# Decay rows laid out chunk by chunk, and another order of the opening, of the loads and of two blocks

## The chip, the cores and the metric

The kernel runs on one core of a Trainium2 chip. The metric is device time in microseconds (us) of one execution; lower is better. A core has five engines with queues of their own: TensorE (PE; its weight loads are shown apart as PEld), VectorE (DVE), ScalarE (ACT), GpSimd (POOL) and SyncE (SP), which here only issues DMAs. Line numbers are those of the kernel before.

## The reference

A Mamba-2 scan over 32 pairs of batch and head (4 batches, 8 heads, 768 tokens, 32 channels, 16 states), followed by a feed-forward layer with a maximum over three products. The scan is written with chunks; what one chunk computes, with `cum` the running sum of the logarithms of `a`:

```python
L = np.exp(cum[:, :, :, None] - cum[:, :, None, :]) * causal
M = np.einsum('bhin,bhjn->bhij', Cc, Bc) * L
y = np.einsum('bhij,bhjd->bhid', M, xc) \
  + np.einsum('bhin,bhnd->bhid', Cc, state) * np.exp(cum)[:, :, :, None]
state = decay_full * state + np.sum(Bx, axis=2)
...
x = y.transpose(0, 2, 1, 3).reshape(3072, 256)
h = np.maximum(np.maximum(x @ w1, x @ w2), x @ w3)      # 3072 x 768
out = h @ w_out                                         # 3072 x 256
```

## The kernel before

**Tiling.** The kernel cuts the 768 tokens into 6 chunks of 128 tokens. One chunk of all four batches is 512 columns of the feed-forward part. Chunk c's scan gives `y`, 256 channels by 512 tokens, which is the feed-forward input of chunk c. The scan of chunk c+1 is put between the feed-forward matmuls of chunk c. All matmuls of one engine run in the order in which the program writes them; that order is written out by hand as strings of one-letter words.

**The opening** (the string before line 997) does chunk 0's scan. `C0`, `B0`, `C1`, `B1` transpose halves of C and B (two batches each), `c` and `b` copy them, `i`, `j`, `v` and `u` build the exponent of the decay on TensorE, GpSimd and VectorE, `e` takes its exponential on ScalarE, `s` makes scores, `x` and `z` multiply them with the decay on VectorE, `y` does so for two heads groups through a ScalarE copy and GpSimd (`aside_product`, L894 and L896), `o0` and `o2` make the two halves of y (`first_own`, L631), `A` and `S` the state. `P` is a dummy matmul that keeps TensorE busy. `k`, `l` and `r` clip, take logarithms and sum `a` for all chunks, and `r` ends with `store_sums`, which writes the running sums to the DRAM tensor `cums`. `W` fetches the next of 12 weight pieces of 512 KB, `X0` and `X1` ask for B and C of chunk 1, `L` for its decay rows, `E` for its end-of-chunk rows. `G` and `H` are the two halves (L679) of the first two feed-forward groups.

**The first feed-forward part** (loop `for n in range(NF * 3)`, strings FIRST) has 18 groups in plain float32, two per weight piece; groups 0 and 1 are the halves of the opening, groups 2 to 17 are two matmuls each (L687). A group's result is copied (L1170) or goes into a maximum (L1174). Each weight piece is first decoded (`d`: two ScalarE steps L220 and L229, two VectorE steps L221 and L224, one GpSimd addition L230; `g`: the sign, VectorE L233). Behind group n the words of FIRST[n] are issued: `b` and `t` transpose B and C of the next chunk (TensorE, L511), `C` and `c` make C's copies (L530) and its product with the exponential `E` (L541, after ScalarE's L534), `s0` and `s2` make scores, `p0` takes four pieces of the decay's exponential (ScalarE, L485), `x` multiplies scores with decay (VectorE, L596), `m` masks the decay rows on GpSimd (L478), `w` splits a weight piece for the later, three-term products (L267, L269, L273 or L277, L262), and `M` issues a load: `M10` and `M11` the two decay loads of chunk 1, `M6`, `M7`, `M8` its B, C and x, `M9` its E; `M0`, `M1`, `M2` B, C and x of chunk 2, `M3` its E, `M4` and `M5` its decay loads. `scan_tc` has 32 dummy matmuls (L520) ahead of chunk 1's transposes of C.

**The seam** (SEAM, PRELUDE) makes y of chunk 1 (`scan_own`: 32 matmuls with the state, L611, then 64 with the decayed scores, L620) and splits it into three terms (L647, L650, L661).

**Blocks one to five** have 18 units each (`unit`): two opening matmuls (L728), a scaling of the bank by ScalarE (L714), four main matmuls (L750), then a copy (`COPIES` says which on ScalarE, the others on VectorE, L762) or a maximum (L764). `unit_open` opens units ahead; the units in `LATE` open the next one after their main matmuls, the others before. Block one (SECOND) also has chunk 0's down projections (`D`, L787) and the scan of chunk 2; blocks two to four (STEADY) have down projections L792; block five (LAST) has no scan left.

**Loads.** All loads but three small ones of `a` go through SP's queue, in program order. The program gives DMAs eight semaphores in turn, and each DMA waits for the one eight places ahead of it. C has one buffer, B and x two each, the decay tiles L two; weight pieces and the split weights share twelve. A decay load copies rows of two batches to all 128 partitions; E is loaded by eight DMAs, one per head:

```python
cums = dram.tile([BH, NC, P], FP32, name="cums")
...
nc.sync.dma_start(
    out=L[:, b:b + 2].rearrange("j b h i -> j (b h) i"),
    in_=cums[b * NH:(b + 2) * NH, c, :].partition_broadcast(P))
```

Of the kernel before, what the change touches and what calls it, by code (L numbers as in the profile page):

```python
# [9 lines left out]
FP32 = mybir.dt.float32  # L10
# [10 lines left out]
def kernel(  # L21
# [55 lines left out]
    COPIES = {c: (1, 6, 7,) if c == 1 else (1, 13,) for c in range(1, NC)}  # L77
    LATE = {c: (2, 3, 5, 8, 10, 14, 16, 17,) if c == 1 else (1, 3, 4, 6, 7, 9, 11, 14, 16, 17,) for c in range(1, NC)}
    WEIGHTS_DVE = ((0, 1), (1, 2), (2, 1), (3, 1), (4, 1), (5, 2), (6, 1), (7, 1), (8, 1), (10, 2), (11, 1), (11, 2),)
# [223 lines left out]
    for word in "W B0 C0 B1 C1 W W x0 x1".split():  # L303
        if word == "W":
            fetch()
        else:
            load_half(word[0], int(word[1]))
# [153 lines left out]
    cums = dram.tile([BH, NC, P], FP32, name="cums")  # L461

    def decay_load(c, pairs=(0, 2)):
        L = decays(c) if 0 in pairs else Ls[c]
        for b in pairs:
            nc.sync.dma_start(
                out=L[:, b:b + 2].rearrange("j b h i -> j (b h) i"),
                in_=cums[b * NH:(b + 2) * NH, c, :].partition_broadcast(P))

    def last_load(c):  # L470
        E = blocks[c]["E"] = raw.tile([HN, NB, P], FP32, tag="E", bufs=2, name="E")
        rows = cums[:, c].rearrange("(b h) s -> h b s", h=NH)
# [42 lines left out]
    def scan_tc(c, kind):  # L515
        st = blocks[c]
        st["trC"] = tr = kind([HN, NB, P], "trC")
        if c == 1:
            for _ in range(32):
                nc.tensor.matmul(  # L520
                    out=tr[:, 0, :64], lhsT=ident16[:, :HN], rhs=mask[:, :64], start=True, stop=True)
# [376 lines left out]
    def store_sums():  # L898
        nc.sync.dma_start(
            out=cums.rearrange("k c s -> (k c) s").rearrange("(w r) s -> r w s", w=2), in_=a_sb)  # L900
# [93 lines left out]
    for word in ("v3 q v2 d i0 j P P P P C0 k e01 e00 c0 J e11 i2 u2 B0 P P B1 b0 e10 P s0 g e20 l "  # L994
            "x0 P P C1 b1 i3 c1 x3 r u3 x2 e30 e31 x1 W P P P s2 s3 e21 D P P A X0 z0 y2 y3 "
            "o0 z1 n d o2 W W N G0 E W H0 G1 H1 S W").split():
        begin(word)
# [71 lines left out]
    def plan(words, c, n):  # L1069
# [9 lines left out]
        "g d",  # L1079
        "W g M10 M7 d",  # L1080
        "",
        "d g d W W",
        "W f",
        "M11 g w0,0 F M3 d M8 g w1,0 m0,0",
        "b",
        "",
        "M0 g",
        "d p0 d M1 t d C g",
        "p0",
        "m0,2 s0 E d",  # L1090
        "p0",
        "w1,1 g w0,1 M2 c M4 x M5",
        "x",
        "p0 x p0 p0 B x",
        "s2 p0 g d g x",
        "p0 w2,0 x x w0,2 x w3,0 g w2,1 w1,2 w2,2",
    ]
    SEAM = "y a z A a D z w3,1 x"
    PRELUDE = "b B w3,2"
    SECOND = [  # L1100
        "t w4,0 E w5,0 c w6,0 w4,1 L m0,0",
        "",
        "p0",
# [118 lines left out]
```

## Time and profile before

| What | us |
|---|---|
| median of 3 runs (lowest, highest) | 275.91 (275.49, 277.44) |
| the profiled execution | 275.21 |
| its span, first to last instruction | 273.5 |

By stage, in one answer of windows (busy us of each engine, granted TensorE clock as a share of full speed, mean busy share of the DMA engines):

| Stage | us from the start | PE | DVE | ACT | POOL | clock | DMA |
|---|---|---|---|---|---|---|---|
| opening | 0 to 21.4 | 18.8 | 10.6 | 12.3 | 8.9 | 1.00 | 0.87 |
| first feed-forward part and seam | 21.4 to 63.7 | 40.0 | 35.7 | 31.5 | 24.1 | 1.00 | 0.96 |
| block one | 63.7 to 102.3 | 38.4 | 26.1 | 33.4 | 26.0 | 1.00 | 0.75 |
| block two | 102.3 to 143.2 | 40.4 | 28.0 | 28.7 | 6.7 | 1.00 | 0.57 |
| blocks three and four | 143.2 to 223.7 | 80.5 | 53.2 | 55.1 | 7.5 | 1.00 | 0.26 |
| block five and the end | 223.7 to 273.5 | 46.6 | 28.8 | 20.6 | 0.0 | 1.00 | 0.07 |

Busy time of TensorE counts the overlapping ends of matmuls as busy, so a stage in which it is busy throughout has no idle time, but not every busy stage is at the peak. A chain of waits follows the end of the program back through what released each step. Idle time of an engine off that chain costs nothing.

### The profile page before, as it was taken

What the parts mean: (1) busy time and instruction counts of PE and PEld (TensorE: products, weight loads), DVE (VectorE), ACT (ScalarE), POOL (GpSimd) and SP (SyncE); (2) the same over time, 40 slices, a digit from 0 to 9 for tenths busy, and PEclk for the clock granted to TensorE, in tenths of its full rate; (3) what the DMA queues carried; (4) which work ended last, traced back from release to release, by engine and by line L of the source; (5) the groups of instructions that cost most, each with busy time, mean ns of one, the idle gap of its engine ahead of it and who ended that gap; (6) DMA issues with size and microseconds to landing.
All of it is one profiled execution on the core that took longest, in us unless ns stands there. A gap on an engine that the chain in (4) does not pass through costs nothing.

```text
span 273.5 us, 5483 instructions
## 1 busy us (share of the span) xinstructions
PE 264.7 (97%) x2100; PEld 206.7 (76%) x2100; DVE 182.4 (67%) x297; ACT 181.6 (66%) x413; POOL 73.0 (27%) x72
## 2 busy tenths in 40 slices
PE   6999999989999999999999999999999999999995
PEld 4566444448877788679888889788789788899894
DVE  2574979798556689862588861688761787732882
ACT  3768759963998998936689845699754564534711
POOL 4433566574949270133001133001000000000000
PEclk9999999999999999999999999999999999999999
DMA  5999799599993175994304794200000100002002
GB/s 123 176 193 224 245 240 312 117 110 213 288 250 57 50 94 75 153 250 41 99 19 40 141 230 53 79 2 0 0 4 29 49 2 2 0 0 79 0 0 77
DMA packets 105097, 28.13 MB, mean 103 GB/s; under 512 B 75376, under 2 KB 102000, under 8 KB 105072
## 3 DMA queue, kind: packets, MB, share of 16 engines
q1 hardware_dynamic: 104768, 27.66, 48.9%
q8 instruction: 16, 0.26, 0.4%
q10 hardware_dynamic: 304, 0.13, 0.2%
q14 instruction: 9, 0.07, 0.1%
HBM read 24.54 MB, written 3.24 MB: 102 GB/s over the span
## 4 chain that ended last, share of the span: by engine, by line
PE 81%; DVE 7%; ACT 5%; DMA 4%; issue 2%; POOL 1%; ACTq 0%; DVEq 0%; POOLq 0%
PE up L750 26%; PE up L728 13%; PE o L792 13%; PE up L687 6%; DMA raw_C<-in_C_dram 4%; PE s L588 4%; PE o L787 4%; PE y L620 3%; PE o L819 2%; PE spread L414 2%; ACT L L485 2%; PE y L611 2%; PE up L679 1%; PE up L914 1%; DVE L L596 1%
## 5 line engine op out<-in xcount | busy, mean ns | idle before, releaser
L750 PE MATMUL up<-six,wp 128*128 128x512 f32 x360 | 96.5, 396 | 0.5 <-ACT up L714 0.5
L750 PEld LDWEIGHTS up<-six,wp 128*128 128x128 f32 x360 | 66.0, 188 | 16.0 <-ACT up L714 1.4
L764 DVE TENSOR_TENSOR m<-m,up 128x512 f32<-128x512 f32 x60 | 40.4, 683 | 48.2 <-PE up L750 47.9
L714 ACT ACTIVATE up<-up 128x512 f32<-128x512 f32 x90 | 50.7, 581 | 26.7 <-PE up L728 25.5
L485 ACT ACTIVATE L<-L,ncums 128x128 f32<-128x128 f32 x160 | 50.3, 393 | 2.4 <-POOL L L478 2.3
L728 PE MATMUL up<-six,wd 128*128 128x512 f32 x180 | 51.7, 394 | 0.0
L728 PEld LDWEIGHTS up<-six,wd 128*128 128x128 f32 x180 | 33.1, 188 | 8.5 <-DVE m L764 1.0
L596 DVE TENSOR_TENSOR L<-s,L 128x512 f32<-128x512 f32 x46 | 30.3, 682 | 2.4 <-PE s L588 1.6
L478 POOL TENSOR_SCALAR_AFFINE_SELECT L<-L 128x1024 f32<-128x1024 f32 x20 | 22.7, 1161 | 26.8 <-DMA L<-cums 26.8
L687 PE MATMUL up<-six,w 128*128 128x512 f32 x64 | 28.7, 596 | 0.0
L792 PE MATMUL o<-wp,h 128*128 128x256 f32 x192 | 23.7, 283 | 0.0
L792 PEld LDWEIGHTS o<-wp,h 128*128 128x128 f32 x192 | 23.4, 192 | 0.1
L661 DVE SCALAR_TENSOR_TENSOR h<-h,h 128x512 fp32r<-128x512 f32 x30 | 21.5, 718 | 1.0
L687 PEld LDWEIGHTS up<-six,w 128*128 128x128 f32 x64 | 11.8, 190 | 13.1 <-issue 11.6
L667 ACT ACTIVATE h<-m 128x512 fp32r<-128x512 f32 x30 | 18.4, 628 | 3.6 <-DVE m L764 3.6
L670 DVE TENSOR_TENSOR h<-m,h 128x512 fp32r<-128x512 f32 x30 | 20.5, 683 | 0.1
L230 POOL TENSOR_TENSOR h<-h,h 128x512 uint32<-128x512 uint32 x12 | 16.7, 1392 | 13.9 <-DVE h L224 9.6
L762 DVE COPY m<-up 128x512 f32<-128x512 f32 x19 | 13.1, 688 | 9.8 <-PE up L750 9.6
L805 ACT ACTIVATE ob<-o 128x512 f32<-128x512 f32 x10 | 6.0, 598 | 19.9 <-PE o L792 16.2
L588 PE MATMUL s<-six,six 32*128 32x256 f32 x192 | 15.4, 401 | 0.0
L575 POOL TENSOR_TENSOR S<-S,old 128x256 f32<-128x256 f32 x4 | 2.9, 736 | 44.7 <-DVE S L567 44.7
L588 PEld LDWEIGHTS s<-six,six 32*128 32x128 f32 x192 | 9.7, 184 | 5.9 <-issue 3.1
(111 smaller groups left out, 324.2 us busy)
## 6 DMA issues: line engine op xcount, KB each, us to landing
L<-cums SPq DMA_DIRECT2D x10, 1024.0 KB, 10.0
rb<-in_moe_w_dram SPq DMA_DIRECT2D x9, 512.0 KB, 5.1
raw_x<-in_x_dram SPq DMA_DIRECT2D x5, 512.0 KB, 10.3
out_dram<-ob SPq DMA_DIRECT2D x10, 256.0 KB, 2.1
rb<-in_moe_w_out_dram SPq DMA_DIRECT2D x3, 512.0 KB, 7.1
raw_B<-in_B_dram SPq DMA_DIRECT2D x5, 256.0 KB, 5.7
E<-cums SPq DMA_DIRECT2D x40, 32.0 KB, 2.2
raw_C<-in_C_dram SPq DMA_DIRECT2D x5, 256.0 KB, 6.5
```

Of the source, the lines that this page charges most:

```text
L478: nc.gpsimd.affine_select(out=Ls[c][:, b], in_=Ls[c][:, b], pattern=[[0, NH], [1, P]], compare_op=ALU.is_ge, fill=MASKED, base=0, channel_ ...
L485: nc.scalar.activation(L[:, b, h], L[:, b, h], AF.Exp, bias=ncum[c][:, b * NH + h:b * NH + h + 1], scale=1.0)
L588: nc.tensor.matmul(out=s[:, i].rearrange("j g i -> j (g i)"), lhsT=st["BT"][rows, b], rhs=st["CT"][rows, :, b], start=(i == 0), stop=True, ...
L596: nc.vector.tensor_tensor(out=M, in0=s, in1=M, op=ALU.mult)
L661: nc.vector.scalar_tensor_tensor(out=out, in0=lo.bitcast(FP32), scalar=-1.0 / TAU, in1=hi.bitcast(FP32), op0=ALU.mult, op1=ALU.add)
L670: nc.vector.tensor_tensor(out=lo, in0=src, in1=hi.bitcast(FP32), op=ALU.subtract)
L687: nc.tensor.matmul(out=bank, lhsT=whole[3 * (f // 2) + i][:, k, f % 2 * P:(f % 2 + 1) * P], rhs=yT[0][:, k], start=(k == 0), stop=(k == KD ...
L714: nc.scalar.activation(bank, bank, AF.Copy, scale=-KAPPA)
L728: nc.tensor.matmul(out=o, lhsT=weight_part(k, 2, kk, cols), rhs=yT[c][2][:, kk], start=(kk == 0), stop=(kk == KD - 1), skip_group_check=True)
L750: nc.tensor.matmul(out=o, lhsT=weight_part(k, j, kk, cols), rhs=yT[c][j][:, kk], start=False, stop=(kk == KD - 1 and j == 1), skip_group_c ...
L764: nc.vector.tensor_tensor(out=m[g], in0=m[g], in1=o, op=ALU.max)
L792: nc.tensor.matmul(out=o[:, b % 2], lhsT=hs[f][p][:, tokens(b)], rhs=weight_part(NW + f // 2, p, f % 2, slice(0, DM)), start=(first and p ...
```

## The change

`cums` is laid out chunk by chunk, so that what one decay load reads is one run of 8 KB instead of 16 rows of 512 bytes; it is stored by two DMAs instead of one. The order of the first loads changes (C ahead of B, x ahead of two of the first four weights). The opening, FIRST, the seam and SECOND get other orders: C of chunk 1 is asked for in the opening, right after B and one weight; its two decay loads follow four weights later, E of chunk 1 comes behind eleven weights and both decay loads, and then one decay load, the last weight, x of chunk 1, B, C, x and the second decay load of chunk 2, and its E. The transposes of chunk 1's B go ahead of group 2, those of C behind group 4. The 32 dummy matmuls of `scan_tc` are gone; the opening has 13 dummies (`P`) instead of 14. Which units open late, which copies go to ScalarE and which weight splits to VectorE changes too; STEADY and LAST keep their words.

```diff
-    COPIES = {c: (1, 6, 7,) if c == 1 else (1, 13,) for c in range(1, NC)}
-    LATE = {c: (2, 3, 5, 8, 10, 14, 16, 17,) if c == 1 else (1, 3, 4, 6, 7, 9, 11, 14, 16, 17,) for c in range(1, NC)}
-    WEIGHTS_DVE = ((0, 1), (1, 2), (2, 1), (3, 1), (4, 1), (5, 2), (6, 1), (7, 1), (8, 1), (10, 2), (11, 1), (11, 2),)
+    COPIES = {c: (7, 12,) if c == 1 else (1, 12, 13,) for c in range(1, NC)}
+    LATE = {c: (3, 5, 9, 10, 11, 13, 15, 16,) if c == 1 else (1, 3, 4, 6, 7, 8, 10, 12, 13, 14, 16, 17,) for c in range(1, NC)}
+    WEIGHTS_DVE = ((0, 1), (1, 1), (2, 1), (3, 1), (4, 1), (6, 1), (6, 2), (7, 1), (8, 2), (9, 1), (10, 1), (10, 2),)
...
-    for word in "W B0 C0 B1 C1 W W x0 x1".split():
+    for word in "C0 W B0 C1 B1 x0 W x1 W W".split():
...
-    cums = dram.tile([BH, NC, P], FP32, name="cums")
+    cums = dram.tile([NC, BH, P], FP32, name="cums")
...
-                in_=cums[b * NH:(b + 2) * NH, c, :].partition_broadcast(P))
+                in_=cums[c, b * NH:(b + 2) * NH].partition_broadcast(P))
...
-        rows = cums[:, c].rearrange("(b h) s -> h b s", h=NH)
+        rows = cums[c].rearrange("(b h) s -> h b s", h=NH)
...
-        if c == 1:
-            for _ in range(32):
-                nc.tensor.matmul(
-                    out=tr[:, 0, :64], lhsT=ident16[:, :HN], rhs=mask[:, :64], start=True, stop=True)
         transposes(tr, st["C"])
...
-        nc.sync.dma_start(
-            out=cums.rearrange("k c s -> (k c) s").rearrange("(w r) s -> r w s", w=2), in_=a_sb)
+        for w in range(2):
+            nc.sync.dma_start(
+                out=cums[:, w * BH // 2:(w + 1) * BH // 2].rearrange("c k s -> k c s"), in_=a_sb[:, w])
...
-    for word in ("v3 q v2 d i0 j P P P P C0 k e01 e00 c0 J e11 i2 u2 B0 P P B1 b0 e10 P s0 g e20 l "
-            "x0 P P C1 b1 i3 c1 x3 r u3 x2 e30 e31 x1 W P P P s2 s3 e21 D P P A X0 z0 y2 y3 "
-            "o0 z1 n d o2 W W N G0 E W H0 G1 H1 S W").split():
+    for word in ("k P q i2 C0 v2 v3 P c0 d i0 B0 j P P P u2 J l b0 P e01 P e10 e00 e11 s0 C1 e21 g "
+            "r x2 B1 c1 P P i3 b1 s3 P x3 e20 P D P s2 x1 u3 e30 X0 e31 x0 y2 y3 W P X1 W W "
+            "z0 z1 o0 d n A W G0 o2 G1 S W N L0 H0 H1").split():
...
     FIRST = [
-        "g d",
-        "W g M10 M7 d",
-        "",
-        "d g d W W",
-        "W f",
-        "M11 g w0,0 F M3 d M8 g w1,0 m0,0",
-        "b",
-        "",
-        "M0 g",
-        "d p0 d M1 t d C g",
-        "p0",
-        "m0,2 s0 E d",
-        "p0",
-        "w1,1 g w0,1 M2 c M4 x M5",
-        "x",
-        "p0 x p0 p0 B x",
-        "s2 p0 g d g x",
-        "p0 w2,0 x x w0,2 x w3,0 g w2,1 w1,2 w2,2",
+        "M11 g W d d f",
+        "W g b",
+        "d g",
+        "",
+        "d t",
+        "F d g w0,0",
+        "g m0,0 g",
+        "",
+        "C w1,0",
+        "w1,1 s0 d d p0",
+        "",
+        "M9 g d p0 p0 p0 g",
+        "M4 w2,0 E W m0,2 x M8 x",
+        "M0 w0,1 x c",
+        "d w3,0 w2,1 x p0 p0",
+        "d",
+        "w0,2",
+        "w1,2 p0 M1 B p0 s2 M2 x x w2,2 M5 M3 g x g x g",
     ]
-    SEAM = "y a z A a D z w3,1 x"
-    PRELUDE = "b B w3,2"
+    SEAM = "y a z a A z w3,1 D x"
+    PRELUDE = "b w3,2 B"
     SECOND = [
-        "t w4,0 E w5,0 c w6,0 w4,1 L m0,0",
-        "",
-        "p0",
-        "C w5,1 p0",
-        "w7,0 D",
-        "s0 h w6,1 w8,0 w9,0 w4,2",
-        "m0,2 w7,1 m1,2 p0 r x x",
-        "h D p0 w5,2",
-        "p0 w6,2 w7,2 p0",
-        "D w10,0 x x",
-        "r s2 p0 w8,1 w9,1 w11,0 m1,0 w8,2 w9,2 x p0",
...
+        "t C E m0,0 w4,0 D p0 w4,1",
+        "w4,2",
+        "w5,0",
+        "w6,0",
+        "p0 w5,1 c w7,0 L",
+        "p0 h p0 w8,0 w5,2 s0 x h x w7,1 m0,2 p0 m1,2 p0",
+        "w6,1 D D",
+        "w6,2 x w9,0 w7,2 w10,0 r m1,0 x",
+        "",
+        "p0 w8,1 p0 w8,2 r s2",
...
```

## The prediction

> **What bounds the kernel now.** I read the chain of waits first. It is 81% TensorE, so a change pays only where TensorE stands still, and I looked for those places in TensorE's timeline (columns: start us, length, engine, line, what, count; in brackets the idle time ahead and what ended it).
>
> ```profile
> 39.49 1.10 PE L520 MATMUL trC<-mask,ident 128*128 128x64 bf16 x32
> 41.64 0.66 PE L511 MATMUL trC<-ident,raw_C 128*128 128x128 f32 x4 [1.05 <-DMA raw_C<-in_C_dram]
> ...
> 57.04 1.98 PE L687 MATMUL up<-six,w 128*128 128x512 f32 x4
> 59.45 0.43 PE L611 MATMUL y<-six,S 32*64 32x128 f32 x4 [0.43 <-DVE L L596]
> 60.73 1.09 PE L611 MATMUL y<-six,S 32*64 32x128 f32 x28 [0.85 <-DVE L L596]
> 61.75 1.95 PE L620 MATMUL y<-L,raw_x 128*32 128x128 f32 x64
> ```
>
> Two holes: 1.10 us of dummies plus 1.05 us of waiting ahead of chunk 1's transposes of C, and VectorE's late decay products (L596) ahead of chunk 1's y. Why C is late stands in SyncE's queue:
>
> ```profile
> 29.66 0.47 SPq L466 DMA_DIRECT2D L<-cums  x1
> 30.22 4.74 SPq L148 DMA_DIRECT2D raw_C<-in_C_dram  x1
> 35.01 6.09 SPq L195 DMA_DIRECT2D rb<-in_moe_w_out_dram  x3
> 41.15 0.47 SPq L466 DMA_DIRECT2D L<-cums  x1
> 41.66 10.07 SPq L474 DMA_DIRECT2D E<-cums  x8
> 51.77 0.43 SPq L148 DMA_DIRECT2D raw_x<-in_x_dram  x1
> ```
>
> C is asked for at 30.22, behind a decay load of 1 MB, and lands at 41.6. From block two on nothing is left: the starts of y on the chain are one TensorE-filled period of 40.24 us apart.
>
> ```profile
> 141.34 1.88 PE y L620 x64
> ...
> 181.58 1.88 PE y L620 x64
> ...
> 221.82 1.88 PE y L620 x64
> ```
>
> DMA speed is in windows of 2 us (after the engines: clock, DMA share, GB/s): weights in 1 KB runs, then decay rows in 512-byte runs.
>
> ```profile
> 32.00:34.00 2.00, 2.00 (x8) 0.99 (x7) 1.97 (x4) 1.72 (x4) 1.09 (x2) 1.00 1.05 405
> 74.00:76.00 2.00, 2.00 (x11) 1.67 (x10) 0.93 (x2) 2.00 (x6) 2.00 (x3) 1.00 1.20 291
> ```
>
> **What the Trainium skill says.** "DMA: Bandwidth & Descriptors", Specifications, puts line rate at runs of 512 bytes and more, under a ceiling of 435 GB/s. The trace disagrees on the first: 291 GB/s at 512 bytes, 405 at 1 KB. Its section on queues has each DMA engine consume its ring in order; the trace agrees: a 256 KB load that takes 4.0 us alone (at 143.73) took 11.4 us behind the decay rows. "TensorE: Matmul & The Clock Gate", Part 2, keeps matmuls in program order, so a transpose that waits stops all groups behind it; 41.64 shows it. Its Part 1 has the clock fall after about 3.4 us of idleness; the granted clock is 1.00 in all windows of 5 us, and the new order leaves no such gap that I can see.
>
> **The change, part by part** (times of the changed kernel are estimates, built from rows of this trace).
>
> *Opening, -1.05 us.* Now the first whole group (L687) starts at 25.12, and the transposes of chunk 1's B (0.44) come later, at 33.90: 25.56 together. In the new order two of the eight half-group matmuls (0.95 us) stand ahead of y's second half, which waits for GpSimd's two products (L896, 18.03 to 20.55) anyway. GpSimd's input, the copies of scores (L894), I put 0.3 us earlier, since their scores no longer trail. So: products done 20.2, y to 21.2, the other six half-group matmuls 2.85, B 0.44: 24.5. Spoiler: B must land by 24.05. It lands at 23.6 now with the same set of loads ahead of it; its queue is moved (x earlier, two W later), not lengthened; the rows' store is two DMAs instead of one (0.45 us more on SP). Bounds: -2 (y earlier by another us) and 0 (B late).
>
> *C ahead of its rows, -2.15 us.* In the queue C follows B and one weight: 23.6 + 1.4 + 2.4 (1.9 and 2.7 are the steps of C in this queue) = 27.4. It is needed after three whole groups, 24.5 + 3 x 1.72 = 29.7. So the wait (1.05) and the dummies (1.10) go. What is next: VectorE's decoding of weights; following its new order with 1.2 us per decode on ScalarE, 1.5 on VectorE and 1.3 on GpSimd, each weight is done 0.9 us or more ahead of its group. The tightest is weight 2: the first group's copy ends at 23.6, ScalarE's decode of weight 2 and of weight 3 at 25.9, VectorE's four steps for both at 26.3, GpSimd's addition at 26.4, the sign at 27.1; group 4 wants it at 24.5 + 2 x 1.72 = 27.9. The one buffer of C delays nothing: the load waits for the last transposes of chunk 0's C, at 13.4 now, before SP gets to it. Bounds: -2.15 and -1.1 (dummies alone).
>
> *The seam, -0.7 us.* Now the last group ends at 59.02 and y at 63.7: 4.68 us for 3.0 of matmuls. In the new order the last scores come after the last group: 24.5 + 16 x 1.72 + 0.75 (small transposes) + 2 x 1.43 (scores with the refill of 0.35) = 55.6. Behind them VectorE has four products and two signs of weights, 6 x 0.6 = 3.6 us, and y's last quarter 0.4: 59.6, that is 4.0 us after the scores. Decay rows land before 40 rather than at 38.9 and 51.2, so ScalarE's exponentials (32 x 0.31 us) no longer bunch up at 50.96 to 55.8. Bounds: -1.7 (no VectorE stall) and +1 (the signs wait for GpSimd).
>
> With 0.2 of rounding y ends at 59.6 instead of 63.7: -4.1. State, down projection and transposes that follow (3.6 us) stay.
>
> *Rows of 8 KB.* A decay load steps the queue by 3.5 us now (landings at 70.6, 74.1, 77.7 and 81.3); at the weights' rate, 1.05 MB / 405 = 2.6 us. Bounds: 2.4 (the page's ceiling) and, above, 3.5 (runs are split) or more: all 128 descriptors then read the very same 8 KB, which no row shows. None of it lies on TensorE's path; it matters for what stands behind it in the one queue. E of chunk 1 moved from 22.70 to behind eleven weights and both decay loads (its exponential is wanted near 47, it lands near 45); E of chunk 2, eight issues of 0.42 us, moved from 41.66 to behind all that chunk 2 loads. Tally after C (27.4): four weights 5.6, two L 5.2, two weights 4.0; then eight E issues, the last of which waits for a DMA eight places ahead (eight semaphores in turn; that is why E took 10.07 us at 41.66), and the next L arrives 5.2 later: 47.4. One weight 2.0, x 3.7, B 2.1, C 1.9, x 3.8, L 2.6: 63.5; E's last 2.7: 66.2. Taken instead from the landing of the same set now (74.1 with two idle stretches of 1.9, one of which goes, and four faster L) I get 68.7. Who waits: E's exponential in block one's first step on ScalarE, wanted at 67.8; behind it a weight split, on which VectorE's next split and copies wait in order, and four exponentials, then the scaling of a unit that TensorE wants about 1.5 us later. So nothing up to 69.3, then 1 us per us. From the two tallies 66.2 to 68.7 I take +0.3; the bounds are 0 and, with L at 3.5 (E 3.6 later), +3.
>
> *Units.* LATE only swaps a unit's two opening matmuls with the four main ones of the unit ahead, the same two units being open after each; COPIES moves one copy of 0.6 us per block to ScalarE. The 40.24 us are full: 0, bounds -0.3 and +0.3 for each of five blocks. Block one keeps its four down steps; its state matmuls go behind y. Its stalls now are small (0.28 at 83.6, 0.46 at 113.1): 0, bounds -0.9 and +1.5.
>
> Sum: -1.05 - 2.15 - 0.7 - 0.2 + 0.3 = -3.8 us. The profiled execution took 275.21 us (span 273.5 and 1.7 around it); that gives 271.4. The median shown, 275.91, is 0.7 above it: **272.1**.
>
> **Rivals.**
> *Slower: the common 8 KB.* Should reads of one place by all engines be slow, each L costs 4 x its excess at E, since four L stand ahead. From 67.4 (middle of the two tallies, with L at 2.6) the slack of 1.9 ends at L = 3.1 us; the gain is gone at 4.0, and at 5 us the time is 275.9 + 4 = 280. For it: no row shows 8 KB that all engines read together; now each load spreads over 48 KB. Against: the rows of 512 bytes are shared by 128 partitions too and run at 291 GB/s. 0.11.
> *The gain is given back in block one* (same or just faster). L stays at 3.5, or x of chunk 1, which I have landing at 53 to 56 against 56.7, comes late, or ScalarE's exponentials queue ahead of unit scalings: 1 to 3 us back, 274.2. For: of the nine windows of 5 us from 70 to 115, five have ScalarE or VectorE busy for 4.9 or more. 0.22. That the rows don't become one run is within this.
> *More:* the seam at full worth and block one's stalls gone, 1.0 + 0.9 more: 270.2. Against: VectorE has 4.9 of 5 us in the seam now. 0.12.
>
> **How the numbers follow.** Forecast 0.55 at 272.1, its own range 270.8 to 273.5. Range over cases: 270.0 leaves out 0.05 below, 276.0 about 0.13 above. One per cent, 2.76 us, is about what a measurement can tell from no change: faster means under 273.15, which is 0.85 of the forecast, all of "more" and a little of the second rival: 0.62; slower, over 278.7: 0.10; the rest 0.28.
>
> **What would show it.** The first whole group at about 24.5; C's transposes with no wait, near 29.7; y of chunk 1 ending near 59.6; L landing 3 us after its turn, SP's issues of it short; E's exponential of chunk 2 near 68 with no DMA wait over 1 us; then the old period of 40.24. Wrong would be: TensorE idle behind DMA at B, C or x of chunk 1; windows with L alone at under 250 GB/s; a period over 40.5.

## The result, and the profile after

| | kernel before | changed kernel |
|---|---|---|
| median, us (13 runs each, same chip) | 276.1 (274.85 to 279.9) | 274.58 (274.25 to 275.45) |
| ratio | | 0.9952, 95% interval 0.9931 to 0.9973 |
| span of the profiled execution, us | 273.5 | 272.8 |
| TensorE busy, us | 264.7 | 264.9 |
| share of the chain: TensorE, DMA | 81%, 4% | 87%, 1% |
| bulk DMA queue, share of 16 engines | 48.9% | 45.5% |
| packets | 105,097 | 85,913 |

The forecast was 272.1 us, 3.8 less than before. About 1.3 us came (0.48% of 276.1); between the two profiled spans it is 0.7 us instead of 3.8. The direction was right and the size was not, so the question is where some 3 us of the span went.

I cut both spans at one point that both kernels pass: the start of the first whole group of chunk 0's FFN once chunk 1's B is transposed (25.12 + 0.44 = 25.56 before, as in the prediction). The cut splits the answer cleanly.

| stretch, us | before | forecast | changed kernel |
|---|---|---|---|
| start to first whole group | 25.56 | 24.5 | 27.33 |
| from there to the end of chunk 1's y | 38.1 | 35.1 | 36.6 |
| from there to the end of the span | 209.8 | 210.1 | 208.9 |

Behind the opening the change is worth 2.5 us (247.9 to 245.5), where the forecast had 2.75. The opening, which should have given 1.05, cost 1.8.

First the part that came as forecast. TensorE's timeline of the changed kernel, in the columns of the prediction:

```profile
33.01 0.60 PE L511 MATMUL trC<-ident,raw_C 128*128 128x128 f32 x4
```

No dummies, and no bracket with a wait: C's transposes follow the group ahead of them. Why is in SyncE's queue:

```profile
22.39 0.42 SPq L148 DMA_DIRECT2D raw_C<-in_C_dram  x1
22.86 6.24 SPq L195 DMA_DIRECT2D rb<-in_moe_w_dram  x4
29.14 1.09 SPq L466 DMA_DIRECT2D L<-cums  x2
...
31.29 13.32 SPq L474 DMA_DIRECT2D E<-cums  x8
```

C is issued at 22.39 instead of 30.22, ahead of both decay loads, and the eight loads of E are the ones that stand in the queue for 13 us, where no engine waits for them. The 8 KB rows move about as fast as I had priced them. A window of the changed kernel in which two decay loads run, every packet of payload in it one row of 8 KB (after the engines: granted clock, DMA share, GB/s):

```profile
77.00:78.00 1.00, 1.00 (x6) 0.84 (x5) 0.37 (x1) 0.87 (x2) 1.00 (x1) 1.00 0.98 393
```

393 GB/s stands where the kernel before had 291. (The 405 of the prediction's window was put down to weights in runs of 1 KB; that window's packets, in the trace, are of 2 KB.) The median time from a decay load's issue to its landing fell from 10.0 to 7.3 us. The starts of y on the chain of waits still lie one period of 40.24 us apart:

```profile
139.55 1.03 PE y L607 x32
...
179.79 1.03 PE y L607 x32
...
220.03 1.03 PE y L607 x32
```

The seam came short. TensorE's timeline there:

```profile
57.33 1.15 PE L584 MATMUL s<-six,six 32*128 32x256 f32 x16
59.59 0.43 PE L607 MATMUL y<-six,S 32*64 32x128 f32 x4 [1.11 <-DVE L L592]
60.18 1.09 PE L607 MATMUL y<-six,S 32*64 32x128 f32 x28 [0.16 <-DVE L L592]
61.20 1.72 PE L616 MATMUL y<-L,raw_x 128*32 128x128 f32 x52
63.29 0.62 PE L616 MATMUL y<-L,raw_x 128*32 128x128 f32 x11 [0.37 <-DVE L L592]
```

The scores end at 58.48 and y at 63.9: 5.4 us where I had put 4.0. All three waits are for VectorE's decay products.

Now the opening. The kernel before, TensorE's timeline:

```profile
4.41 2.17 PE L414 MATMUL spread<-a,pick 32*128 32x128 f32 x32
6.28 1.40 PE L426 MATMUL spread<-npick,a 32*128 32x512 f32 x8
7.60 1.04 PE L914 MATMUL up<-mask,ident 128*128 128x512 bf16 x4
...
11.89 1.15 PE L588 MATMUL s<-six,six 32*128 32x256 f32 x16
```

The changed kernel:

```profile
4.69 0.61 PE L911 MATMUL up<-mask,ident 128*128 128x512 bf16 x1
5.23 2.08 PE L414 MATMUL spread<-a,pick 32*128 32x128 f32 x16
7.24 0.69 PE L511 MATMUL tr<-ident,raw_C 128*128 128x128 f32 x2
7.72 0.63 PE L911 MATMUL up<-mask,ident 128*128 128x512 bf16 x1
8.28 2.09 PE L414 MATMUL spread<-a,pick 32*128 32x128 f32 x32
...
11.89 0.82 PE L911 MATMUL up<-mask,ident 128*128 128x512 bf16 x3
...
13.36 1.88 PE L584 MATMUL s<-six,six 32*128 32x256 f32 x16
```

No bracket stands in either. Look at one instruction in both instead: the padding matmul of 128x512 bf16 (L914, L911). One by one it is recorded with 0.61 to 0.63 us while TensorE is slow and 0.38 to 0.39 once it is fast; behind one another their starts lie 0.43 and 0.22 us apart, so slow is half the rate. Before, it is fast at 7.60. In the changed kernel it is still slow at 7.72 and fast at 11.89, and the transposes (0.47 us slow, 0.27 fast) put the change near 10.6. The profile's windows give a granted clock of 1.00 for all of this time, in both kernels. But the record of the clock that the trace keeps begins only at 6.92 us before and at 10.65 in the changed kernel, with full clock; the profile's windows count what lies ahead of its first entry as 1.00. With the slow start the scores s0 begin 1.47 us later. That fits: 3.73 us more at half rate lose about 1.9 us (an estimate), and some 0.3 us of B's transposes moved from ahead of s0 to behind it.

The timeline hides one thing more. The 16 matmuls of s0 take 1.88 us in the changed kernel and 1.15 before, both at full rate. A matmul's recorded end is modelled and reaches over the next start, so a short wait gets no bracket, and a stage that counts as busy throughout can hold such waits. The row of the weight loads (PEld) shows them:

```profile
13.36 0.56 PEld L584 LDWEIGHTS s<-six,six 32*128 32x128 f32 x6 [0.42 <-ACT L L446]
14.11 0.72 PEld L584 LDWEIGHTS s<-six,six 32*128 32x128 f32 x10 [0.20 <-ACT L L446]
```

L446 is ScalarE's exponentials; in the kernel before the four that s0 comes behind are done at 11.74, ahead of it.

### The profile page after: what moved, and what is told of

Read it like the earlier page. It is cut to its first block, busy times and chain, and to the rows that moved or that the text cites. A ratio compares the mean times of both kernels' runs of the same rounds, so it can differ in the third digit from the quotient of the medians.

```text
span 272.8 us, 5404 instructions
## 1 busy us (share of the span) xinstructions
PE 264.9 (97%) x2067; PEld 206.6 (76%) x2067; DVE 184.2 (68%) x294; ACT 182.6 (67%) x415; POOL 75.4 (28%) x72
## 2 busy tenths in 40 slices
DMA packets 85913, 28.13 MB, mean 103 GB/s; under 512 B 75392, under 2 KB 81536, under 8 KB 84608
## 3 DMA queue, kind: packets, MB, share of 16 engines
q1 hardware_dynamic: 85584, 27.66, 45.5%
## 4 chain that ended last, share of the span: by engine, by line
PE 87%; DVE 6%; ACT 3%; issue 1%; DMA 1%; ACTq 0%; DVEq 0%
PE up L746 30%; PE up L724 15%; PE o L788 13%; PE up L683 5%; PE s L584 5%; PE o L783 4%; PE y L616 3%; PE o L815 2%; PE spread L414 2%; DVE L L592 2%; PE y L607 2%; PE up L911 1%; PE up L675 1%; DVE w L233 1%; ACT L L485 1%
## 5 line engine op out<-in xcount | busy, mean ns | idle before, releaser
L746 PE MATMUL up<-six,wp 128*128 128x512 f32 x360 | 93.9, 393 | 0.3 <-ACT up L710 0.3
L710 ACT ACTIVATE up<-up 128x512 f32<-128x512 f32 x90 | 51.5, 584 | 25.6 <-PE up L724 25.3
L724 PE MATMUL up<-six,wd 128*128 128x512 f32 x180 | 54.1, 398 | 0.0
L592 DVE TENSOR_TENSOR L<-s,L 128x512 f32<-128x512 f32 x46 | 30.2, 683 | 2.1 <-PE s L584 1.2
L478 POOL TENSOR_SCALAR_AFFINE_SELECT L<-L 128x1024 f32<-128x1024 f32 x20 | 24.1, 1230 | 14.9 <-DMA L<-cums 14.9
L758 DVE COPY m<-up 128x512 f32<-128x512 f32 x16 | 11.0, 687 | 8.6 <-PE up L746 8.6
L584 PE MATMUL s<-six,six 32*128 32x256 f32 x192 | 15.7, 401 | 0.0
L262 POOL TENSOR_TENSOR wd<-wp 128x512 fp32r<-128x512 f32 x9 | 13.2, 1473 | 7.6 <-PE up L746 6.2
```

The source lines that it names most:

```text
L478: nc.gpsimd.affine_select(out=Ls[c][:, b], in_=Ls[c][:, b], pattern=[[0, NH], [1, P]], compare_op=ALU.is_ge, fill=MASKED, base=0, channel_ ...
L584: nc.tensor.matmul(out=s[:, i].rearrange("j g i -> j (g i)"), lhsT=st["BT"][rows, b], rhs=st["CT"][rows, :, b], start=(i == 0), stop=True, ...
L592: nc.vector.tensor_tensor(out=M, in0=s, in1=M, op=ALU.mult)
L710: nc.scalar.activation(bank, bank, AF.Copy, scale=-KAPPA)
L724: nc.tensor.matmul(out=o, lhsT=weight_part(k, 2, kk, cols), rhs=yT[c][2][:, kk], start=(kk == 0), stop=(kk == KD - 1), skip_group_check=True)
L746: nc.tensor.matmul(out=o, lhsT=weight_part(k, j, kk, cols), rhs=yT[c][j][:, kk], start=False, stop=(kk == KD - 1 and j == 1), skip_group_c ...
```

## The experiments

The prediction's steps give three questions: what the opening lost, whether C, rows and order stand alone, and what the seam's VectorE costs. For each profiled run the table has the time from which the clock record of its trace shows full clock (for e11, which has no record, the time at which the durations change), the starts of s0 and of the first whole group, and what remains of the span after it. It is one run for each kernel, and some kernels differ from run to run, as will be seen.

| kernel | full clock from | s0 | first whole group | span less that |
|---|---|---|---|---|
| before | 6.9 | 11.89 | 25.56 | 247.9 |
| changed | 10.6 | 13.36 | 27.33 | 245.5 |
| e5 old opening | 8.3 | 12.49 | 26.09 | 244.9 |
| e1 first sums first | 6.3 | 12.35 | 26.80 | 245.4 |
| e2 i0 first | 7.2 | 12.44 | 26.41 | 245.4 |
| e6 exponentials first | 8.6 | 13.49 | 27.46 | 245.4 |
| e12 more pads | 5.9 | 11.90 | 25.87 | 245.4 |
| e13 pads moved | 6.2 | 11.34 | 26.03 | 245.4 |
| e14 half pads | 14.1 | 14.88 | 29.57 | 245.4 |
| e10 i0 and s2 first | 15.7 | 15.68 | 29.21 | 245.5 |
| e11 s2 first | 13.1 | 14.49 | 28.46 | 245.4 |
| e17 both early | 7.8 | 12.98 | 26.95 | 245.4 |
| e15 old opening, pads first | 7.9 | 12.57 | 26.18 | 244.9 |
| e16 before, pads first | 6.7 | 11.95 | 25.76 | 247.9 |
| e3 signs last | 12.0 | 13.99 | 27.98 | 245.9 |
| e7 short rows | 12.9 | 14.32 | 28.27 | 246.9 |
| e9 before, long rows | 7.2 | 12.02 | 25.61 | 248.9 |
| e8 before, long rows, C ahead | 7.8 | 12.38 | 25.99 | 250.8 |

(For kernels with the old FIRST list the transposes of chunk 1's B, 0.44, are added to the group's start.) The last column answers one question for all: with the rest of the changed kernel untouched it is 245.4 or 245.5, however early or late the opening ends. What the opening loses arrives at the end in full.

Four rows answer another. The changed kernel, e3, e7 and e11 have the same words up to s0, and full clock came at 10.6, 12.0, 12.9 and 13.1. Their s0 stands at 13.36, 13.99, 14.32 and 14.49: close to half a microsecond later for each microsecond of half rate, with no change of order.

**Is it the opening? e5** puts the opening of the kernel before into the changed kernel.

```diff
-    for word in "C0 W B0 C1 B1 x0 W x1 W W".split():
+    for word in "W B0 C0 B1 C1 W W x0 x1".split():
...
-    for word in ("k P q i2 C0 v2 v3 P c0 d i0 B0 j P P P u2 J l b0 P e01 P e10 e00 e11 s0 C1 e21 g "
-            "r x2 B1 c1 P P i3 b1 s3 P x3 e20 P D P s2 x1 u3 e30 X0 e31 x0 y2 y3 W P X1 W W "
-            "z0 z1 o0 d n A W G0 o2 G1 S W N L0 H0 H1").split():
+    for word in ("v3 q v2 d i0 j P P P P C0 k e01 e00 c0 J e11 i2 u2 B0 P P B1 b0 e10 P s0 g e20 l "
+            "x0 P P C1 b1 i3 c1 x3 r u3 x2 e30 e31 x1 W P P P s2 s3 e21 D P P A X0 z0 y2 y3 "
+            "W o0 X1 z1 n d o2 W W N G0 W H0 G1 H1 S W L0").split():
```

> The changed kernel with the whole opening of the kernel before (its order of the first loads and of the words; chunk 1's B, C and rows stay in the changed order behind it). Theory 'the opening lost what the rest won': the first exponentials start at 7.8 again, the first whole group at 25.1 to 25.6 instead of 27.33, all behind it follows one to one: 272.6 to 273 us, ratio to the kernel before 0.988. Rival 'the rest lives on the late opening' (weights or C of chunk 1 not there in time): the first whole group is early, but TensorE then waits on ScalarE's or VectorE's decoding or on chunk 1's C before 60, and the ratio stays at 0.995 or more.

Measured: 272.95 us, ratio 0.9897 (0.9848 to 0.9945). The first whole group stands at 26.09, and the rest follows. This is the first theory; it is also faster than both kernels (the intervals of e5 and of the changed kernel overlap a little; e15 below repeats the value). So the rest of the change never needed its new opening.

**Order, or rate? e1, e2, e6.** e1 takes the first sums ahead of everything, e2 only i0 (j, which the exponentials wait for, stays behind), e6 adds the exponentials.

```diff
-    for word in ("k P q i2 C0 v2 v3 P c0 d i0 B0 j P P P u2 J l b0 P e01 P e10 e00 e11 s0 C1 e21 g "
+    for word in ("k P q i0 j v2 v3 i2 C0 P c0 d B0 P P P u2 J l b0 P e01 P e10 e00 e11 s0 C1 e21 g "
```

> The changed kernel with the first sums (i0, j) back ahead of i2 and C0 in the opening. Theory 'opening order': ScalarE's first exponentials (L446) start near 7.9 us instead of 11.99, the first whole group (L683) near 24.7 instead of 27.33, and the end follows: about 2.6 us under the changed kernel, ratio to the kernel before near 0.986. Rival 'VectorE bounds the seam whatever the opening does': the first whole group is early all the same, but y of chunk 1 (L616) still ends at 63.2 or later and the ratio stays near 0.995.

```diff
-    for word in ("k P q i2 C0 v2 v3 P c0 d i0 B0 j P P P u2 J l b0 P e01 P e10 e00 e11 s0 C1 e21 g "
+    for word in ("k P q i0 i2 C0 v2 v3 P c0 d B0 j P P P u2 J l b0 P e01 P e10 e00 e11 s0 C1 e21 g "
```

> Only i0 goes ahead of i2 and C0; j, which the exponentials wait for, stays behind both. Theory 'slow array': the 128-row i0 in place of the 64-row i2 lets TensorE reach its full rate near 7.5 us as in the kernel before (a padding matmul of 128x512 bf16 then takes 0.27 us and not 0.6), the scores s0 start about 1.5 us earlier (11.9 instead of 13.36) and the end is 1 to 1.5 us under the changed kernel. Rival 'order alone': full rate comes at 10.4 as now or the exponentials still start near 11 and nothing is gained; first whole group at 27 or later.

```diff
-    for word in ("k P q i2 C0 v2 v3 P c0 d i0 B0 j P P P u2 J l b0 P e01 P e10 e00 e11 s0 C1 e21 g "
+    for word in ("k P q i0 j v2 v3 e01 e00 i2 C0 P c0 d B0 P P P u2 J l b0 P P e10 e11 s0 C1 e21 g "
```

> As e1 (i0 and j ahead of i2 and C0), and on ScalarE the first two exponentials now go ahead of the copies of C and B and of the decoding. Theory 'ScalarE's order held e1 back' (there the exponentials could start at 7.8 and started at 11.47, behind c0, d, l and b0): they start near 7.8 and the scores s0 lose 0.5 to 0.9 us, first whole group near 26 (e1: 26.80), end 0.5 to 0.9 us under e1. Rival 'the later chain sets it' (products, second half's scores, GpSimd): the first whole group stays at 26.8.

Measured: e1 274.18 us, 0.9954 (0.9938 to 0.997); e2 273.5 us, 0.9941 (0.9913 to 0.9968); e6 273.97 us, 0.9932 (0.9905 to 0.9959). e1 missed its 2.6 us: its exponentials start at 11.47, because ScalarE has them behind the copy of C, a decoding, a logarithm and the copy of B. e6 cleared that (they start at 8.96), and in its profiled run, with full clock from 8.6, the first whole group was no earlier (27.46); that run took 274.59 us, above its median. e2 hit the mechanism: with i0 in front TensorE is fast from 7.2, and s0 starts 0.92 earlier, though j and with it the exponentials keep their place behind i2 and C0. By the ratios e1, e2 and e6 are worth 0, 0.3 and 0.6 us against the changed kernel, less than the intervals can tell; e2's average hides two groups of runs. So the order of the opening's work is worth little by itself, and the rate more.

**What makes TensorE slow for longer? e12, e13, e14.** i2 works on 64 of the 128 rows of the array (two tiles of 32), i0 on all 128. e12 adds three full padding matmuls ahead of i2, e13 moves them there from behind j, and e14 is e13 with 64 rows.

```diff
-    for word in ("k P q i2 C0 v2 v3 P c0 d i0 B0 j P P P u2 J l b0 P e01 P e10 e00 e11 s0 C1 e21 g "
+    for word in ("k P P P P q i2 C0 v2 v3 P c0 d i0 B0 j P P P u2 J l b0 P e01 P e10 e00 e11 s0 C1 e21 g "
```

> The changed kernel with three more padding matmuls (128 rows each, 0.6 us each while TensorE is slow) ahead of i2. Theory 'a half-filled array does not raise the clock, a full one does': full rate near 7.5 to 9 us and not 10.4; i2 (64 rows) itself then runs at full rate in part, and the scores s0 come at 13.3 to 13.9 in spite of 1.8 us of added work. Rival 'the number of us, not the rows, decides, and i2 has no part in it': full rate at 10.4 or later as in the changed kernel and s0 1.8 us later, near 15.2.

```diff
-    for word in ("k P q i2 C0 v2 v3 P c0 d i0 B0 j P P P u2 J l b0 P e01 P e10 e00 e11 s0 C1 e21 g "
+    for word in ("k P P P P q i2 C0 v2 v3 P c0 d i0 B0 j u2 J l b0 P e01 P e10 e00 e11 s0 C1 e21 g "
```

> The changed kernel with three padding matmuls moved from behind j to ahead of i2, none added. Theory 'slow start': full rate near 5.6 to 7 us instead of 10.5, s0 near 11.9, first whole group near 25.9, end 1.4 to 2 us under the changed kernel: ratio to the kernel before 0.988 to 0.990. Rival 'order of work': the single run of e12 was lucky, full rate comes at 9 or later in most runs, and the ratio stays at 0.994 to 0.996.

```diff
-            out=halves[0].rearrange("p (k i) -> p k i", i=P), lhsT=ident16,
-            rhs=mask.unsqueeze(1).to_broadcast([P, NB, P]), start=True, stop=True)
+            out=halves[0].rearrange("p (k i) -> p k i", i=P), lhsT=ident16[0:rows],
+            rhs=mask[0:rows].unsqueeze(1).to_broadcast([rows, NB, P]), start=True, stop=True)
...
+        elif op == "Q":
+            pad(P // 2)
...
-    for word in ("k P q i2 C0 v2 v3 P c0 d i0 B0 j P P P u2 J l b0 P e01 P e10 e00 e11 s0 C1 e21 g "
+    for word in ("k Q Q Q Q q i2 C0 v2 v3 P c0 d i0 B0 j u2 J l b0 P e01 P e10 e00 e11 s0 C1 e21 g "
```

> As e13, but the four padding matmuls ahead of i2 use 64 rows of the array, as i2 does, and not 128. Theory 'rows in use count': TensorE's rate does not rise before 9 to 13 us, as in the changed kernel, and the time stays within 0.5 us of it (ratio 0.994 to 0.997). Rival 'matmuls in flight count, rows do not': full rate at 5.6 to 7 as in e13 and the same time as e13.

Measured: e12 273.05 us in its one run. Its TensorE timeline:

```profile
4.60 1.68 PE L911 MATMUL up<-mask,ident 128*128 128x512 bf16 x4
6.21 1.16 PE L414 MATMUL spread<-a,pick 32*128 32x128 f32 x16
...
11.90 1.88 PE L584 MATMUL s<-six,six 32*128 32x256 f32 x16
```

The same i2 takes 1.16 us and not 2.08, and s0 starts 1.46 earlier with 1.1 us of work added. e14, with half-filled padding:

```profile
4.61 1.88 PE L911 MATMUL up<-mask,ident 64*128 64x512 bf16 x4
6.42 2.07 PE L414 MATMUL spread<-a,pick 32*128 32x128 f32 x16
...
9.47 2.09 PE L414 MATMUL spread<-a,pick 32*128 32x128 f32 x32
```

All is slow up to 14.05, and its 14 runs took 275.31 to 276.86 us (ratio 1.0026, 1.0006 to 1.0047), none as little as e13's better ones. That speaks against "matmuls in flight count, rows do not", on two good runs of five against none of fourteen. For e13 is no clean win: five runs, 272.99 and 273.14 and then 276.67 to 276.86; ratio 1.001 (0.9949 to 1.0071). Its profile is of a 273.14 run. e2 and e10 fall into two groups in the same way (e2: thirteen runs of 272.9 to 273.9 and seven of 275.8 to 277.3). The profiled run of e2 is of its faster group, with full clock from 7.2; that of e10 is of its slower group, with full clock from 15.7, though the words are the same up to s0. So full matmuls in front bring the fast rate early in some runs only, and in the others it comes later than in the changed kernel (for e13 no such run was profiled).

The Trainium skill, "TensorE: Matmul & The Clock Gate", Part 1, describes a half rate at the start, lifted after a window of some 3.4 us of sustained work, with windows that run free of the kernel's start. The traces agree on the half rate (starts 0.43 apart against 0.22) and on the length of the clock's window: in every trace with a record the stretches at full clock are whole multiples of 3.413 us, 78 of them before and 77 in the changed kernel. TensorE's first matmul starts at 2.5, so the first of these windows that lies wholly behind it ends between 5.9 and 9.3. In there full clock came in all seven kernels with before's opening (6.7 to 8.8, e4 among them) and in e1, e2, e6, e12, e13 and e17. With i2 in front and one padding matmul ahead of it it came at 10.6 to 13.1 in four kernels, a window later or more. The page does not speak of rows in use; e13 against e14 does. That a window filled mostly by i2 does not count is my reading of these times and is not shown: e10, with i0 in front, was late too. In e2 and e10 TensorE also stands still for 0.71 and 0.50 us ahead of B's transposes, and no run tells such a wait from the rows.

**Pads first in the old order: e15, e16.** e15 is e5, e16 the kernel before, each with four padding matmuls moved ahead of i0.

```diff
-    for word in ("v3 q v2 d i0 j P P P P C0 k e01 e00 c0 J e11 i2 u2 B0 P P B1 b0 e10 P s0 g e20 l "
+    for word in ("v3 q v2 d P P P P i0 j C0 k e01 e00 c0 J e11 i2 u2 B0 P P B1 b0 e10 P s0 g e20 l "
```

> As e5 (opening of the kernel before, rest of the changed one), with its four padding matmuls moved from behind j to ahead of i0. Theory 'slow start': full rate near 5.6 to 7 instead of 8.2, i0 and j take 2.3 us and not 4, first whole group 0.3 to 0.8 us earlier than in e5 (26.09), ratio 0.986 to 0.989. Rival 'nothing left to gain there': j ends where it did, ScalarE's exponentials start at 8.3 again, ratio as e5, 0.990.

> The kernel before with the same move. Theory 'slow start': full rate at 5.6 to 7 and not at 7.3 to 9.1, 0.2 to 0.8 us faster, and less spread between runs: ratio 0.997 to 0.999. Rival: the pads only push i0 and j back, ratio 1.000 to 1.003.

Measured: e15 273.04 us, 0.9908 (0.9883 to 0.9932), the same as e5; e16 275.85 us, 1.0002 (0.998 to 1.0024). Nothing gained in either, with full clock from 7.9 and 6.7 against 8.3 and 6.9: the old opening has i0, on all rows, in front anyway. e16's runs spread no less than those of the kernel before (274.16 to 281.22).

**The stretch from s0 to the first whole group: e11, e10, e17.** It was forecast at 24.5 - 11.89 = 12.6 and is 13.97. In the changed kernel s2, which GpSimd's products wait for, comes behind s3 and three padding matmuls. e11 swaps s2 and s3, e10 does so in e2, e17 in e6.

```diff
-            "r x2 B1 c1 P P i3 b1 s3 P x3 e20 P D P s2 x1 u3 e30 X0 e31 x0 y2 y3 W P X1 W W "
+            "r x2 B1 c1 P P i3 b1 s2 P x3 e20 P D P s3 x1 u3 e30 X0 e31 x0 y2 y3 W P X1 W W "
```

> The same swap of s2 and s3 alone in the changed kernel. By the theory of e10 the first whole group stands 13.4 us or less after s0 and the end is 0.4 to 1 us under the changed kernel (ratio 0.992 to 0.994), TensorE's slow start left as it is; by the rival nothing changes.

> As e2 (i0 ahead of i2 and C0), and the scores s2, which GpSimd's two products wait for, go ahead of s3 and of three padding matmuls. Theory 's2 behind s3 is the second half of the opening's loss': ScalarE's copies of s2 start 0.6 us or more earlier after s0 than the 6.6 us of e2 and of the changed kernel, GpSimd's products and y's second half follow, the first whole group stands 13.4 us or less after s0 (now 13.97), and the end is 0.4 to 1 us under e2. Rival 'ScalarE's exponentials or VectorE set the products': 13.97 us as before, end as e2.

> e6 (first sums and first two exponentials early) and the swap of s2 and s3 together. Theory 'two limits side by side' (the exponentials of the second half, and s2 standing behind s3 and three padding matmuls): with both moved GpSimd's products start 0.6 to 1.2 us earlier after s0, the first whole group stands 12.9 to 13.5 us after s0 instead of 13.97, end 0.4 to 1 us under e6 (273.97). Rival 'TensorE's own work fills the stretch': 13.9 to 14 us again, end as e6.

Measured: e11 274.51 us, 0.9967 (0.9944 to 0.999); e10 275.94 us, 0.9969 (0.9939 to 0.9999), nine runs of 273.1 to 273.9 and eleven of 275.9 to 276.8; e17 274.13 us, 0.9948 (0.9931 to 0.9965). The stretch is 13.97 in e11 and in e17. In e17 GpSimd's products are finished at 21.59 and y's second half starts at 22.81, behind the two half-groups. In e10 it is 13.53 with the same matmuls: its exponentials were done before its late s0, which then takes 1.08 us up to the next matmul, where the changed kernel takes 1.81. The rival holds but for this: **TensorE's own work fills all of the stretch but 0.44 us**, which goes to waits for ScalarE and VectorE that have no bracket, and bringing GpSimd's products forward does not make it shorter.

**C ahead of its rows, alone: e4, e8.** In the kernel before, without the dummies; e8 with 8 KB rows as well.

```diff
-        if c == 1:
-            for _ in range(32):
-                nc.tensor.matmul(
-                    out=tr[:, 0, :64], lhsT=ident16[:, :HN], rhs=mask[:, :64], start=True, stop=True)
...
-        "W g M10 M7 d",
+        "W g M7 M10 d",
```

> The kernel before with one part of the change: chunk 1's C loads ahead of its decay rows, and the 32 dummies go. Theory of the prediction: 1.10 us of dummies and 1.05 us of wait vanish and 2.15 us arrive at the end, ratio 0.992. Rival 'the seam takes it back': the decay rows land later still (51.2 and on), ScalarE's exponentials and VectorE's products of chunk 1 do not move, so the last groups are earlier but y of chunk 1 ends at 63 or later; gain under 0.7 us, ratio 0.998 or above.

> The kernel before with C ahead of its rows, no dummies and rows of 8 KB (e4 with long rows). Theory 'rows and order of C belong together': L lands 3 to 5 us earlier than in e4, ScalarE stops for less than 1 us, TensorE's 3.9 us wait ahead of chunk 1's scores goes, and the part of the change is worth 1 to 2.15 us: ratio 0.992 to 0.997. Rival 'C ahead of the rows costs in that order of words whatever the rows' (L behind C by a whole load): ratio over 1.005.

Measured: e4 285.31 us, 1.0224 (1.0176 to 1.0272); e8 281.9 us, 1.0241 (1.017 to 1.0312). Neither theory; the rival's sign, and more than either had. ScalarE's timeline of e4, and then TensorE's:

```profile
43.57 1.28 ACT L485 ACTIVATE L<-L,ncums 128x128 f32<-128x128 f32 x4 [4.75 <-POOL L L478]
```

```profile
40.33 0.60 PE L511 MATMUL trC<-ident,raw_C 128*128 128x128 f32 x4
...
48.27 2.09 PE L584 MATMUL s<-six,six 32*128 32x256 f32 x16 [3.90 <-ACT six L526]
```

C is transposed at 40.33 with no wait, as wanted. But in the old list ScalarE's first exponentials (p0) stand ahead of C's scaling (L526). They now wait for rows that land behind C, the scaling waits with them, and the scores idle 3.90 us (2.96 in e8). In e8, whose profiled run keeps full clock once it has it, C ahead of its rows costs 1.9 us against e9, the same kernel with C behind them and with the dummies (250.8 less 248.9). So the term of 2.15 us is not a property of the load order; the new list has the word C ahead of p0.

e4 lost more than the wait. TensorE stands still a second time in its profiled run, 4.92 us among the state's matmuls (68.79 to 73.71; the trace names no cause), and around the two waits the granted clock is 0.50, from 46.40 to 53.22 and from 73.70 to 77.11. That is two windows and one of 3.413 us; the 2.09 us of the scores above, 1.15 in e8, lie in the first. For this its span is left out of the table.

**The rows: e7, e9.** e7 is the changed kernel with rows of 512 bytes (E's reads and the store as before, too), e9 the kernel before with 8 KB rows.

```diff
-    cums = dram.tile([NC, BH, P], FP32, name="cums")
+    cums = dram.tile([BH, NC, P], FP32, name="cums")
...
-                in_=cums[c, b * NH:(b + 2) * NH].partition_broadcast(P))
+                in_=cums[b * NH:(b + 2) * NH, c, :].partition_broadcast(P))
```

> The changed kernel with the rows of 512 bytes again (layout and store as before). Theory of the prediction, rows worth nothing by themselves as long as they land in time: L takes 3.5 us of the queue each again, E of chunk 2 up to 3.6 us later, 0 to 3 us slower. Rival 'the changed order needs the fast rows': the decay rows of chunk 1 land so late that ScalarE stops on the exponentials with C's scaling queued behind them; TensorE idles for several us ahead of chunk 1's scores, 5 us slower or more, ratio over 1.01.

> The kernel before with rows of 8 KB and nothing else. Theory 'the rows are worth what stands behind them in the queue': each L takes about 0.9 us less of the queue, chunk 1's C behind it lands about 1 us earlier and its 1.05 us wait at 41.64 goes; at the seam part of it is lost again to VectorE: 0.3 to 1 us faster, ratio 0.996 to 0.999. Rival 'no effect in that order': C lands when it did (the weights behind it take the queue), ratio 1.000; second rival 'the split store of the rows costs': slower by the 0.5 to 3 us that its second DMA holds SP, ratio over 1.002.

Measured: e7 276.83 us, 1.0016 (0.999 to 1.0041); e9 276.24 us, 1.0021 (1.0006 to 1.0037). In the changed order the rows are worth 1.4 us (246.9 less 245.5 in the last column). This is the cost that the prediction's bound of +3 was for. ScalarE in e7, and TensorE behind it:

```profile
74.48 0.63 ACT L530 ACTIVATE E<-E 128x512 f32<-128x512 f32 x1 [1.85 <-DMA E<-cums]
```

```profile
77.82 1.20 PE L746 MATMUL up<-six,wp 128*128 128x512 f32 x4 [1.13 <-ACT up L710]
```

With fast rows E's exponential in the changed kernel starts at 71.59 with no wait for it. In the old order the same rows cost 1.0 us in the profiled runs (248.9 against 247.9; 0.4 in the medians, 276.24 against 275.83); I had expected that sign only from the split store. GpSimd's timeline of e9, and then TensorE's:

```profile
75.50 4.21 POOL L478 TENSOR_SCALAR_AFFINE_SELECT L<-L 128x1024 f32<-128x1024 f32 x4
80.44 3.30 POOL L262 TENSOR_TENSOR wd<-wp 128x512 fp32r<-128x512 f32 x2 [0.72 <-DVE wp L273]
```

```profile
84.95 2.86 PE L787 MATMUL o<-w,h 128*128 128x256 f32 x12 [1.49 <-DVE L L596]
```

Rows that land earlier let GpSimd do all four masks in one go, before its two weight splits (L262) and not between them. The splits then run at 80.44 to 83.74, beside VectorE, which takes 1.79 us for a subtraction (L670) that took 0.68 before. Its decay products come a microsecond later, and TensorE waits 1.49 instead of 0.18.

**The seam: e3** puts two decay products ahead of the three signs of weights.

```diff
-        "w1,2 p0 M1 B p0 s2 M2 x x w2,2 M5 M3 g x g x g",
+        "w1,2 p0 M1 B p0 s2 M2 x x w2,2 M5 M3 x x g g g",
```

> In the seam the last two decay products go ahead of the three signs of weights on VectorE. Theory 'VectorE's signs delay y': the last decay product ends near 61.3 instead of 63.2, y of chunk 1 loses its 0.37 us wait at 63.29 and ends near 63.2; the first down products (L783) then wait for the last sign near 64.1, so no more than 0.2 to 0.7 us comes of it. Rival 'TensorE's time from the scores on is set elsewhere': y ends where it does now, within 0.2 us.

Measured: 275.37 us, 0.9988 (0.9964 to 1.0013). The wait at y's last quarter goes; from the end of the scores to the end of y it is 4.7 us instead of 5.4. Then VectorE's split of y is late, TensorE's timeline:

```profile
68.74 1.43 PE L724 MATMUL up<-six,wd 128*128 128x512 f32 x5 [0.76 <-DVE six L657]
```

By the last column it costs 0.4 us in all. VectorE's timeline has no idle time between 56 and 67 in the changed kernel, so this order only moved the wait.

## Why the prediction was wrong, step by step

*Opening, -1.05 us: this step failed.* It was +1.77, a miss of 2.83 where the whole span missed by 3.1 (272.8 against 269.7). It falls into two terms.

The first, 1.47 us, is TensorE's slow start: full clock at 10.65 us instead of 6.92. The prediction looked at it and dismissed it: "the granted clock is 1.00 in all windows of 5 us, and the new order leaves no such gap that I can see". I asked only when a fast array turns slow, not when it first turns fast, and I read the clock of the profile's windows, which count the time without a record as full. That the late full clock costs the time is shown by the four kernels with the same opening. Why it comes late is less sure: the change puts i2, on half the rows, where i0 and j had filled the array; e12 and e13's better runs give the term back, e2's better runs much of it, and e14 keeps it, but the same kernels' other runs do not give it back.

The second, 1.36 us, is the forecast's packing. "Two of the eight half-group matmuls stand ahead of y's second half, which waits for GpSimd's two products anyway" counted on idle time. The timeline before has no bracket between 11.89 and 25.12, and y's second half starts at 20.34, straight behind the work ahead of it: TensorE was all but full, with seven padding matmuls of which the change keeps six. The stretch, with chunk 1's B, took 13.67 before and 13.97 after. Two transposes of chunk 0's B moved into it (0.2), about what the dropped padding matmul gave; s0's wait for the exponentials, 0.44 by e10, the prediction put at nothing. The other 0.9 no run gave. e11 and e17 show that bringing the products forward does not shorten it.

*C ahead of its rows, -2.15 us: right in size* (27.33 to the scores' end at 58.48 is 31.15, forecast 31.1), though one group waits 0.29 us at 31.22 for a weight's decoding, where the prediction had every weight 0.9 us or more early. But I had listed the term as a property of the load order. e4 and e8 show that it rests on C's scaling coming ahead of the exponentials on ScalarE, which the prediction did not name.

*The seam, -0.7 us: mis-sized by 1.4.* I counted six VectorE instructions of 0.6 us. The two signs ahead of the last product took 0.90 and 1.17 with GpSimd at work beside them, VectorE was 0.4 behind when the scores ended, and y ended 0.67 after the last product, not 0.4. So the seam cost 0.7 us instead of giving it.

*Rows of 8 KB: right.* 393 GB/s against an assumed 405 (measured on runs of 2 KB, not of 1 KB); E's exponential waits for nothing; E late (+0.3) did not happen. e7 shows what they prevent, 1.4 us.

*Units and block one, 0: 0.9 better,* at the edge of the bound of -0.9. Of it 0.37 are waits that went (0.18, which the prediction read as 0.28, and 0.46 before, 0.27 after); the rest sits in matmuls of units that are recorded a few ns shorter, and I did not test it.

*Rivals.* The common 8 KB was refuted by 393 GB/s. "The gain is given back in block one" came near in its total, 274.2 against 274.58, by luck: block one gained, and the gain was lost in the first 27 us and at the seam.

## What to carry to other kernels

A stretch in which the timeline shows no wait has little to give to a reordering (0.44 of 13.97 us here); before counting on a gap, find its bracket, and look for short waits in the weight loads' row. At the start of a kernel compare the duration of one repeated instruction, not the clock of the profile's windows, and profile several runs: whether full matmuls in front help differed from run to run. When a load is moved ahead of another, look for the engine on which the consumers of both stand in one queue: in e4 and e8 TensorE stood still for 3.90 and 2.96 us by that with the load itself on time.

## What the runs showed of the hardware

TensorE ran at half rate for its first 3 to 13 us of work (0.43 against 0.22 us from one bf16 matmul of 128x512 to the next). The clock record of the traces begins only behind that, and its stretches at full clock are whole multiples of 3.413 us. Four such matmuls on 128 rows ahead of i2 ended the half rate by 6.2 us in the profiled runs of e12 and e13; on 64 rows it lasted to 14.05. It can differ between runs of the same words: full clock came at 7.2 in e2 and at 15.7 in e10, and the times of both lie in two groups about 3 us apart. With waits of 3.90 and 4.92 us e4 fell back to half rate for 6.83 and 3.41 us; e8's wait of 2.96 us had no such cost in its profiled run.

Broadcast rows of 8 KB were read at 393 GB/s, against 291 for rows of 512 bytes, though all 128 partitions read the same 8 KB; weights in runs of 2 KB went at 405.

VectorE slowed beside GpSimd when both its inputs were in SBUF. A sign (L233) takes 0.68 us alone and 1.17 in the seam; a decay product with one input in PSUM (L592) took 0.68 throughout. The Trainium skill, "SBUF — State Buffer", section on who interferes with whom, says that a VectorE instruction with two SBUF inputs contends with GpSimd's reads; these rows agree.
